# Gating row transfers by matmuls, and 128 columns of z as the weights of one matmul

## The chip, the cores and the metric

One core of one Trainium2 chip runs the kernel. The metric is the device time of one execution in microseconds (us). Engines: PE (matmul), with its weight loads shown apart as PEld, DVE (vector), ACT (scalar), POOL (GpSimd), SP (which issues most DMAs).

## The reference

A long convolution by FFT over the sequence, then a mixture of experts over the rows of its result.

```python
batch, seq, d_model = (8, 5056, 128)
...
Yf = np.fft.rfft(x, n=2 * S, axis=1) * np.fft.rfft(h, n=2 * S, axis=0)[None]
y = np.fft.irfft(Yf, n=2 * S, axis=1)[:, :S, :]
...
x = y.reshape(B * S, D)                       # 40448 rows of 128
g_idx = np.argmax(x @ w_group, axis=1)        # one of 4 groups
e_idx = np.argmax(xg @ w_expert[g], axis=1)   # one of 4 experts of the group
out[tok] = g_w * e_w * (np.maximum(x @ w1[g, e], 0.0) @ w2[g, e])
```

## The kernel before, in words

The transform of length 2S = 10112 = 158 x 64 is made by matmuls with constant matrices, in three rounds; round 0 holds the filter and two batches, rounds 1 and 2 three batches each (`ROUNDS`, `nu` = 2, 3, 3).

- `stage1(r)` makes the transform over n1 (48 loads, two steps each; L427 in four tiles of 64x64, L433 with 128 columns of weights).
- `groups(r)` takes 40 pairs of frequencies two at a time: `forward` (L531), `multiply` by the filter (L549), `add` (L583), `inverse` over k2 (L599), whose result z is copied by ACT into `zs` (L610, L612) and stored to `zd` in DRAM.
- `side(r)` makes the inverse over n1 from `zd`, in 16 lumps. A lump does four n2: for each n2 and batch u, L734 multiplies 126 rows of `zm` as weights (64 columns, twice: `c` = 0 and 64, one for each half of PE's columns) by 79 moving columns of `ig`; L748 adds the other 32 rows; ACT copies to `yT` (L755). `zs` keeps its columns as (half r, batch u, 64 channels), so the 128 channels of one batch don't lie side by side. Every two lumps there is a group of 8 n2: gate logits (`lm`, `lt`), rows transposed into `rw` (L791, L792), and `gate_math`, which finds each row's place in the array sorted by expert (`posf`, L1003).
- A group of rows is sent to its places in DRAM (`srt`) by 10 or 15 indirect DMAs of 128 rows (L868), issued by POOL. `side` appends them to the list `self.sends`; `send()` takes one out, and it is called at many chosen places in the program. In front of each, one column of `posf` is copied to `pos` on ACT or DVE (L867). This copy lies in its engine's queue at the chosen place, and the transfer waits for it; so it sets the time of the transfer.
- `ffn_steps` are the experts, in blocks of 512 rows of 8 steps: three fp32r matmuls each for `w1` (L1374 to L1376) and `w2` (L1392 to L1394). Results go out by indirect DMAs (L1445), in the blocks of known number (`timed`) behind a copy `at` of their row numbers on ACT (L1443).

`weave` lays the parts into one program by weights: `side(0)` beside round 1, `side(1)` beside round 2, `side(2)` beside the first experts. Each engine runs its instructions in that order. A group's transfers must be issued before its `rw` buffers are used again, two groups later; `rows(0)` issues what is left then. A matmul on f32 data shows in the trace as two weight loads and two matmuls: the 1024 calls of L734 are 2048 records.

Of the kernel before, what the change touches and what calls it, by code (L numbers as in the profile page):

```python
# [232 lines left out]
class Kernel:  # L233
# [5 lines left out]
    def pools(self, ctx):  # L239
        tc = self.tc  # L240
        self.cp = ctx.enter_context(tc.tile_pool(name="cp", bufs=1))
        self.dr = ctx.enter_context(tc.tile_pool(name="dr", bufs=1, space=DRAM))
        self.ctx, self.banks = ctx, ExitStack()
        self.pq = self.banks.enter_context(tc.tile_pool(name="pq", bufs=4, space=PSUM))
        self.turns, self.beside, self.sends, self.tick = 0, "", [], 0
# [136 lines left out]
    def stage1(self, r):  # L382
# [32 lines left out]
        def mm(k):  # L415
# [7 lines left out]
            for j in range(h * QB // 2, (h + 1) * QB // 2):  # L423
                if fold:
                    for b in range(2):
                        for c in range(2):
                            nc.tensor.matmul(  # L427
                                pp[c * 64:c * 64 + 64, b, j * 2 * HALF:(j + 1) * 2 * HALF],
                                lhsT=tiles[i][b * 64:b * 64 + 64, j, c, :], rhs=self.f[b * 64:b * 64 + 64, 0:2 * HALF],
                                start=True, stop=True, tile_position=(b * 64, c * 64),  # L430
                            )
                else:
                    nc.tensor.matmul(  # L433
                        whole[:, j * 256:j * 256 + N1], lhsT=views[i][:, j * 128:j * 128 + 128], rhs=self.f,
                        start=True, stop=True,
                    )
# [34 lines left out]
    def groups(self, r):  # L471
# [42 lines left out]
        def forward(p):  # L514
# [7 lines left out]
            for i, (to, of, w) in enumerate(steps):  # L522
                for b in range(2):
                    rows = slice(b * 64, b * 64 + 64)
                    for c in range(2):
                        k = w[rows, c * 64:c * 64 + 64]
                        if p == 0 and c == 0:
                            k = first[0][rows, 256 + i * 64:320 + i * 64]
                        data = st[rows, min(2 * p + c, NG - 1)].rearrange("p t w -> p (t w)")
                        begin = to == both or p == 0 and i in (0, 2)  # L530
                        nc.tensor.matmul(  # L531
                            px[c * 64:c * 64 + 64, b, to], lhsT=k, rhs=data[:, of],
                            start=begin, stop=i == len(steps) - 1 or p == 0 and i == 1, tile_position=(b * 64, c * 64),
                        )
# [22 lines left out]
        def product(p):  # L557
# [9 lines left out]
            self.send("a")  # L567
# [8 lines left out]
            if r == 2 and p % 2 == 0 and len(self.sends) > 12:  # L576
                self.send("a")
# [9 lines left out]
        def inverse(p):  # L587
# [7 lines left out]
            for part in range(2):  # L595
                wt, k = (cgs[p + LP], 320 - part * 64) if p > 0 else (first[0], part * 128)
                for c in range(n):
                    for h in (0, 64):
                        nc.tensor.matmul(  # L599
# [6 lines left out]
            else:  # L606
                z = cx.tile([128, 2, W], F32, name="zs", bufs=3)
            if pp is None:
                for c in range(n):
                    nc.scalar.copy(out=z[:, c, 0:w], in_=pz[c][:, 0:w])  # L610
            else:
                nc.scalar.copy(out=z[:, 0:n, 0:w], in_=pp[:, 0:n, 0:w])  # L612
# [33 lines left out]
        def step(k):  # L646
# [4 lines left out]
            self.tick += 1  # L651
# [47 lines left out]
    def side(self, r):  # L699
# [27 lines left out]
        def mm(n):  # L727
# [3 lines left out]
            for u in range(nu):  # L731
                for c in (0, 64):
                    k = c * nu + u * HD
                    nc.tensor.matmul(  # L734
                        pys[q][c:c + 64, col(n, u)], lhsT=zms[q][:, n % QB, k:k + 64], rhs=self.ig[:, 0:NH],
                        start=n % QB == 0 and u == 0, stop=False, tile_position=(0, c),
                    )

        def rest(n):

            zt = zts.pop(n // 4)
            for u in range(nu):
                for q in (n // QB, n // QB + 1):
                    k = q % 2 * QB * RT
                    for c in (0, 64):
                        d = c * nu + u * HD
                        both = pys[q][c:c + 64, 0:QB * c1].rearrange("p (i u m) -> p i u m", i=QB, u=nu)[:, :, u]
                        nc.tensor.matmul(  # L748
# [4 lines left out]
            for q in (n // QB, n // QB + 1):  # L753
                k = QB * q % 8 * c1
                nc.scalar.copy(out=self.yT[:, k:k + QB * c1], in_=pys.pop(q)[:, 0:QB * c1])  # L755

        def lump(k):
            def f():
# [8 lines left out]
                rest(4 * k)  # L767

# [9 lines left out]
        def rows(i):  # L778
# [10 lines left out]
            for j in range(n):  # L789
                k = (4 * i + j) * GP  # L790
                nc.tensor.transpose(out=pt[:, j * D:(j + 1) * D], in_=self.yT[:, k:k + GP], identity=self.ident)  # L791
# [38 lines left out]
        for o in range(N2 // 8):  # L830
# [3 lines left out]
            if r < 2:  # L834
# [3 lines left out]
                at.append((t + 4.7, both(lm, lambda: rows(0)), False))  # L838
                at.append((t + 6.4, both(lt, lambda: rows(1)), False))
                at.append((t + 9.5, both(*more), False))  # L840
                at += [(t + 6.5 + 5.6 * k / (NMATH + REST), advance(ops), True) for k in range(NMATH + REST)]
                at.append((t + 12.15, lambda o=o, s=sends: self.sends.extend((8 * r + o, f, self.tick) for f in s), True))
            else:
# [4 lines left out]
                at.append((t + 3, both(lm, lambda: rows(0)), False))  # L848
                at.append((t + 4, both(lt, lambda: rows(1)), False))
                at.append((t + 5, both(*more), False))  # L850
                at += [(t + 4.02 + 3.3 * k / (NMATH + REST2), advance(ops), True) for k in range(NMATH + REST2)]
                at.append((t + 7.4, lambda o=o, s=sends: self.sends.extend((8 * r + o, f, self.tick) for f in s), True))
# [10 lines left out]
    def scatter(self, k, j, p, r, T):  # L863


        def f(copy):
            copy(out=k["pos"][:, j:j + 1], in_=k["posf"][:, j:j + 1])  # L867
# [7 lines left out]
            )  # L875
            self.no_dep(f"scatter_idx{r}", ins)
# [6 lines left out]
    def send(self, eng="v"):  # L883

        if eng == "a":
            eng = "s" if self.sends and self.sends[0][2] < self.tick else "v"
        if self.sends:
            self.sends.pop(0)[1](self.nc.vector.tensor_copy if eng == "v" else self.nc.scalar.copy)
# [5 lines left out]
    def gate_math(self, od, k, t0, T, nu, rest):  # L894
# [105 lines left out]
        posf = tl([], "posf", bufs=2)  # L1000
# [3 lines left out]
        k["posf"] = posf  # L1004
        k["pos"] = cx.tile([128, 15], I32, name="pos", bufs=3)[0:P, 0:T]
        yield
# [353 lines left out]
    def mm1(self, j, i):  # L1360
# [9 lines left out]
        for f in range(i * G, i * G + G):  # L1370
# [5 lines left out]
            nc.tensor.matmul(o, lhsT=wh[:, k:k + 128], rhs=xl, start=False, stop=True)  # L1376
# [7 lines left out]
    def mm2(self, n, i, c, j=None):  # L1384
# [3 lines left out]
        for f in range(i * G, i * G + G):  # L1388
# [5 lines left out]
            nc.tensor.matmul(p, lhsT=wh[:, k:k + 128], rhs=hl, start=False, stop=f == 7)  # L1394
# [43 lines left out]
    def scatter_out(self, n, timed=False):  # L1438

        for ids, o in self.due[:n]:  # L1440
            if timed:
                at = self.fx.tile([128, 1], I32, name="at", bufs=8)
                self.nc.scalar.copy(out=at, in_=ids)  # L1443
                ids = at
# [7 lines left out]
            )  # L1452
            self.no_dep("scatter_out", ins)
# [45 lines left out]
    def ffn_steps(self, j, prev, end):  # L1499
# [22 lines left out]
        def act(at):  # L1522
            for w, k, q in plan:
# [9 lines left out]
                elif q == "o":  # L1533
                    if prev and j < NA - 2 and at in (4, 6):
                        self.put()
                        self.send("s")
# [109 lines left out]
    def run(self):  # L1646
        tc = self.tc
        with ExitStack() as ctx:
            self.pools(ctx)
            with ExitStack() as c2:  # L1650
# [29 lines left out]
                for r in range(3):  # L1680
# [38 lines left out]
                for k, f in enumerate(steps):  # L1719
# [27 lines left out]
                    elif k < 8 * (NA - 2) and k % 8 not in (3, 4, 5, 6):  # L1747
                        add(lambda: self.send("s"))
# [38 lines left out]
```

## Time and profile before

| | |
|---|---|
| median of 3 runs | 1764.83 us |
| lowest and highest | 1753.78 and 1769.3 us |
| profiled execution | 1761.84 us |
| its span, from the first to the last instruction | 1760.3 us |
| mean granted clock of PE | 0.989 of full speed |

The span misses 1.5 us of the profiled execution's time. The stages in the span: round 0 ends near 140 us, round 1 runs from 140 to 400 and round 2 to 690, the experts from there. "Idle" of an engine is put down to what ended it; "issue" means that the profile shows nothing that the engine waited for.

### The profile page before, as it was taken

The page shows a single profiled execution, that of the slowest core. Times are in us where ns is not written, and L with a number is a line of the kernel's source. Part 1 is how long each engine was busy: PE and PEld are TensorE (multiplying, and loading weights), DVE is VectorE, ACT ScalarE, POOL GpSimd, SP SyncE. Part 2 cuts the span into 40 slices and gives each one's busy share as a digit, 9 for nine tenths or more (in the row PEclk, how much of TensorE's full clock was granted, in tenths as well). Part 3 has the DMA queues.
Part 4 walks back from the last instruction along what each step waited for, and adds up shares of the span by engine and source line. Part 5 has one row for each costly group of instructions (what it writes and reads, how often), then busy time and mean ns, then how long its engine had stood idle before and what let it go on. Part 6 is the DMA issues. An engine that isn't in the chain of part 4 may idle for free. (4 is left out here: it accounts for less than half of the span.)

```text
span 1760.3 us, 47512 instructions
## 1 busy us (share of the span) xinstructions
PE 1649.6 (94%) x16576; PEld 1267.6 (72%) x16576; DVE 1317.5 (75%) x2969; ACT 1118.5 (64%) x2645; POOL 763.5 (43%) x730
## 2 busy tenths in 40 slices
PE   8998898988889898999999999999999999999998
PEld 7676745546755554777777777787777877888987
DVE  6554587864567677687787778888788888887888
ACT  5554444443444444677777777677777777776876
POOL 1451232333244445325455545345555555334545
PEclk9999999998999999999999999999999999999999
DMA  7797576766666787676666755476965687555667
GB/s 212 225 289 214 161 230 215 254 204 201 176 199 212 232 242 214 176 187 178 166 177 165 176 151 142 115 177 185 213 171 138 167 216 199 141 135 147 165 159 176
DMA packets 403939, 330.22 MB, mean 188 GB/s; under 512 B 167708, under 2 KB 347425, under 8 KB 403672
## 3 DMA queue, kind: packets, MB, share of 16 engines
q1 hardware_dynamic: 374808, 271.01, 56.9%
q0 software_dynamic: 20608, 41.79, 7.3%
q10 hardware_dynamic: 8256, 14.10, 2.8%
q8 instruction: 139, 2.28, 0.6%
q14 instruction: 128, 1.05, 0.2%
HBM read 208.00 MB, written 96.86 MB: 173 GB/s over the span
## 5 line engine op out<-in xcount | busy, mean ns | idle before, releaser
L868 POOL DMA_INDIRECT srt<-rw,pos x320 | 334.0, 1044 | 491.1 <-ACT pos L867 141.0
L1445 POOL DMA_INDIRECT out<-orow,at x176 | 190.8, 1084 | 237.1 <-ACT at L1443 122.9
L549 DVE TENSOR_TENSOR y<-pp,hg 128x768 f32<-128x768 f32 (+1 forms) x108 | 92.5, 857 | 93.9 <-ACT hg L539 33.4
L1445 POOL DMA_INDIRECT out<-orow,sids x92 | 96.2, 1045 | 114.8 <-DVE orow L1412 89.3
L599 PE MATMUL pp<-y,cg 64*64 64x384 f32 (+1 forms) x1504 | 132.0, 444 | 13.2 <-issue 6.5
L531 PE MATMUL pp<-st,cg 64*64 64x192 f32 (+1 forms) x1588 | 121.5, 404 | 4.0 <-issue 1.9
L755 ACT COPY yT<-py 128x474 f32<-128x474 f32 (+1 forms) x96 | 44.7, 513 | 116.8 <-PE py L748 88.5
L612 ACT COPY zs<-pp 128x768 f32<-128x768 f32 (+1 forms) x106 | 75.6, 714 | 64.5 <-PE pp L599 38.2
L445 DVE TENSOR_TENSOR st<-pp,odd 128x320 f32<-128x320 f32 x96 | 46.9, 489 | 91.4 <-ACT odd L444 87.4
L734 PE MATMUL py<-ig,zm 126*64 126x79 f32 x2048 | 92.3, 237 | 21.6 <-issue 18.8
L734 PEld LDWEIGHTS py<-ig,zm 126*64 126x64 f32 x2048 | 78.9, 137 | 43.1 <-issue 35.1
L599 PEld LDWEIGHTS pp<-y,cg 64*64 64x64 f32 x1504 | 62.4, 132 | 61.5 <-issue 40.2
L1380 DVE SCALAR_TENSOR_TENSOR h3l<-px,h3h 128x512 fp32r<-128x512 f32 (+1 forms) x111 | 74.4, 671 | 40.9 <-ACT h3h L1379 39.1
L1380 DVE SCALAR_TENSOR_TENSOR h0l<-px,h0h 128x512 fp32r<-128x512 f32 (+1 forms) x109 | 73.3, 672 | 37.2 <-ACT h0h L1379 26.5
L531 PEld LDWEIGHTS pp<-st,cg 64*64 64x64 f32 x1588 | 66.5, 133 | 43.5 <-issue 29.6
L1379 ACT ACTIVATE h0h<-px 128x512 fp32r<-128x512 f32 (+1 forms) x109 | 64.0, 587 | 50.8 <-PE px L1376 38.0
L1380 DVE SCALAR_TENSOR_TENSOR h2l<-px,h2h 128x512 fp32r<-128x512 f32 (+1 forms) x112 | 75.3, 672 | 23.8 <-ACT h2h L1379 15.3
L549 DVE TENSOR_TENSOR m<-pp,hg 128x768 f32<-128x768 f32 (+1 forms) x108 | 91.5, 847 | 0.0
L792 ACT COPY rw<-py 128x1024 uint16<-128x1024 uint16 (+1 forms) x88 | 81.1, 938 | 16.1 <-remote 6.8
L1379 ACT ACTIVATE h3h<-px 128x512 fp32r<-128x512 f32 (+1 forms) x111 | 65.3, 589 | 32.4 <-PE px L1376 20.9
L583 POOL TENSOR_TENSOR y<-y,m 128x512 f32<-128x512 f32 x40 | 50.9, 1277 | 77.3 <-DMA hd<-hg 43.0
L1380 DVE SCALAR_TENSOR_TENSOR h1l<-px,h1h 128x512 fp32r<-128x512 f32 (+1 forms) x111 | 74.4, 671 | 11.3 <-issue 7.7
(482 smaller groups left out, 5248.3 us busy)
## 6 DMA issues: line engine op xcount, KB each, us to landing
wr<-in_moe_w SPq DMA_DIRECT2D x373, 256.0 KB
zd<-zs SPq DMA_DIRECT2D x66, 384.0 KB
zm<-zd SPq DMA_DIRECT2D x64, 378.0 KB
cg<-in_c_g SPq DMA_DIRECT2D x106, 224.0 KB
zd<-zs SPq DMA_DIRECT2D x39, 256.0 KB
hg<-hd SPq DMA_DIRECT2D x68, 128.0 KB
xt<-in_x ACTq DMA_DIRECT2D x52, 160.0 KB
zm<-zd SPq DMA_DIRECT2D x32, 252.0 KB
```

Of the source, the lines that this page charges most:

```text
L445: nc.vector.tensor_tensor(out=all_st[:, 0:2 * HALF, d], in0=even, in1=odd, op=ALU.add)
L531: nc.tensor.matmul(px[c * 64:c * 64 + 64, b, to], lhsT=k, rhs=data[:, of], start=begin, stop=i == len(steps) - 1 or p == 0 and i == 1, til ...
L549: nc.vector.tensor_tensor(out=t[:, :, 0:w].rearrange("p t (r u d) -> p t r u d", r=2, u=nu), in0=taken(px, part).unsqueeze(1).broadcast_to ...
L583: (nc.gpsimd if r == 0 else nc.vector).tensor_tensor(out=y[:, :, 0:w], in0=y[:, :, 0:w], in1=m[:, :, 0:w], op=ALU.add)
L599: nc.tensor.matmul(pz[c][h:h + 64, 0:w], lhsT=wt[c * 64:c * 64 + 64, k + h:k + h + 64], rhs=y[c * 64:c * 64 + 64, part, 0:w], start=part = ...
L612: nc.scalar.copy(out=z[:, 0:n, 0:w], in_=pp[:, 0:n, 0:w])
L734: nc.tensor.matmul(pys[q][c:c + 64, col(n, u)], lhsT=zms[q][:, n % QB, k:k + 64], rhs=self.ig[:, 0:NH], start=n % QB == 0 and u == 0, stop ...
L792: nc.scalar.copy(out=od["rw"][i // 2][:, 4 * i % RH:4 * i % RH + n, 0:2 * D].rearrange("p j (h d) -> p j h d", h=2), in_=pt[:, 0:n * D].bi ...
L868: ins = self.nc.gpsimd.indirect_dma_start(out=self.srt, out_offset=bass.IndirectOffsetOnAxis(ap=k["pos"][0:p, j:j + 1], axis=0), in_=k["rw ...
L1379: nc.scalar.activation(out=hh, in_=p, func=AF.Relu)
L1380: nc.vector.scalar_tensor_tensor(out=hl, in0=p, scalar=0.0, in1=hh.bitcast(F32), op0=ALU.max, op1=ALU.subtract)
L1445: ins = self.nc.gpsimd.indirect_dma_start(out=self.a["out"], out_offset=bass.IndirectOffsetOnAxis(ap=ids, axis=0), in_=o, in_offset=None, ...
```

## The change

1. The copies to `pos` and `at` go. `gate_math` writes the places as integers at once. Instead, each indirect DMA gets a dependency on `self.mark`, the last marked matmul in the program at the place of the call (`behind`). Matmuls of stage 1, of `forward` (for the first of two pairs after its first third, for the second at the end), `inverse`, `rest`, `rows` and the experts set the mark.
2. The places of the calls change: in stage 1 of rounds 1 and 2 after every fourth step (it was every second); in `groups` one after each product and one after each second inverse (further ones before); one after each lump and each other large piece of `side`, outside the experts (`beside`).
3. `inverse` lets ACT write z as (batch u, half r, 64 channels), and L734 takes 128 columns of one batch as the weights of one matmul over all of PE's columns. Half as many matmuls and weight loads are issued there.

```diff
@@ groups
             for i, (to, of, w) in enumerate(steps):
+                if i == 1 and p % 2 == 0:
+                    self.mark = last
...
+            if p % 2 == 1:
+                self.mark = last
...
-            self.send("a")
+            self.send()
             yield
             m = multiply(px, p, 1, "m", 2)
...
-            if r == 2 and p % 2 == 0 and len(self.sends) > 12:
-                self.send("a")
...
+            by_unit = z[:, 0:n, 0:w].rearrange("p t (u r d) -> p t r u d", r=2, d=HD)
...
-                nc.scalar.copy(out=z[:, 0:n, 0:w], in_=pp[:, 0:n, 0:w])
+                nc.scalar.copy(
+                    out=by_unit, in_=pp[:, 0:n, 0:w].rearrange("p t (r u d) -> p t r u d", r=2, d=HD)
+                )
...
                     add(p)
-                    if p == k:
-                        self.send("a")
...
-                    if r == 2 or i == 1:
-                        self.send("s")
+                    if i == 1 or len(self.sends) > 20:
+                        self.send()
@@ side
-                for c in (0, 64):
-                    k = c * nu + u * HD
-                    nc.tensor.matmul(
-                        pys[q][c:c + 64, col(n, u)], lhsT=zms[q][:, n % QB, k:k + 64], rhs=self.ig[:, 0:NH],
-                        start=n % QB == 0 and u == 0, stop=False, tile_position=(0, c),
-                    )
+                nc.tensor.matmul(
+                    pys[q][:, col(n, u)], lhsT=zms[q][:, n % QB, u * D:(u + 1) * D], rhs=self.ig[:, 0:NH],
+                    start=n % QB == 0 and u == 0, stop=False,
+                )
...
-                        d = c * nu + u * HD
+                        d = u * D + c
...
+        def beside():
+            if self.beside != "experts":
+                self.send()
...
                 rest(4 * k)
+                beside()
...
-                at.append((t + 4.7, both(lm, lambda: rows(0)), False))
+                at.append((t + 4.7, both(lm, lambda: rows(0), beside), False))
@@ scatter, send
-        def f(copy):
-            copy(out=k["pos"][:, j:j + 1], in_=k["posf"][:, j:j + 1])
+        def f():
             ins = self.nc.gpsimd.indirect_dma_start(
...
+            self.behind(ins)
...
+    def behind(self, ins):
+        if self.mark is not None:
+            info = mybir.DependencyInfo(mybir.DependencyClass.Sync, mybir.DependencyReason.DATA)
+            self.tc.add_manual_dep(ins.ins, self.mark.ins.name, info, reason="transfers are issued one by one")
@@ gate_math
-        nc.vector.tensor_tensor(out=posf, in0=posf, in1=sg, op=ALU.mult)
+        nc.vector.tensor_tensor(out=k["pos"], in0=posf, in1=sg, op=ALU.mult)
@@ scatter_out
-            if timed:
-                at = self.fx.tile([128, 1], I32, name="at", bufs=8)
-                self.nc.scalar.copy(out=at, in_=ids)
-                ids = at
...
+            if timed:
+                self.behind(ins)
@@ run
-                        if r > 0 and k % 2 == 1:
+                        if r > 0 and k % 4 == 1:
                             add(self.send)
...
-                    elif k < 8 * (NA - 2) and k % 8 not in (3, 4, 5, 6):
-                        add(lambda: self.send("s"))
+                    elif k < 8 * (NA - 2) and (k < 8 * (N0 - 2) or k % 8 not in (3, 4, 5, 6)):
+                        add(lambda: self.send())
```

## Rows read from the trace of the kernel before

**Rows 1.** Page, part 1: busy time (share of the span) xinstructions.

```profile
PE 1649.6 (94%) x16576; PEld 1267.6 (72%) x16576; DVE 1317.5 (75%) x2969; ACT 1118.5 (64%) x2645; POOL 763.5 (43%) x730
```

**Rows 2.** Busy time by stage: stretch, its us, engines, granted clock, DMA share, GB/s.

```profile
140.00:420.00 280.00, 249.01 (x4208) 167.02 (x4208) 192.64 (x476) 127.20 (x335) 79.28 (x82) 0.97 0.69 214
420.00:690.00 270.00, 238.03 (x3653) 152.67 (x3646) 179.10 (x451) 124.08 (x338) 113.97 (x111) 0.98 0.70 209
690.00:1060.00 370.00, 360.01 (x2666) 281.54 (x2667) 284.73 (x663) 269.23 (x616) 170.36 (x160) 0.99 0.68 174
1060.00:1600.00 540.00, 523.66 (x2363) 420.98 (x2363) 441.21 (x915) 404.99 (x903) 265.07 (x252) 1.00 0.63 165
```

**Rows 3.** Groups by form: busy us, mean ns, idle before and what ended it.

```profile
L734 PE MATMUL py<-ig,zm 126*64 126x79 f32 x2048 | 92.3, 237 | 21.6 <-issue 18.8 <-ACT rw L792 2.5
```

**Rows 4.** Timeline of PE, two lumps: start, us, instructions (PE's records are pipelined).

```profile
311.42 1.31 PE L734 MATMUL py<-ig,zm 126*64 126x79 f32 x32
...
763.21 0.50 PE L1394 MATMUL pz<-h0l,w2h 128*128 128x512 f32 x1
763.64 1.86 PE L734 MATMUL py<-ig,zm 126*64 126x79 f32 x48
```

**Rows 5.** Weight loads by line: least, median and largest ns, first and last start.

```profile
L734 PEld LDWEIGHTS py<-ig,zm x2048: 132/137/231, 154.0 to 1049.5; 126*64 126x64 f32 x187
...
L433 PEld LDWEIGHTS pp<-f,xt x288: 186/190/338, 6.5 to 490.4; 128*128 128x128 f32 x144
```

**Rows 6.** Timeline of PEld, the first two 128-column loads of one step.

```profile
18.30 0.30 PEld L433 LDWEIGHTS pp<-f,xy 128*128 128x128 f32 x2
```

**Rows 7.** Timeline of PE: fp32r matmuls with 128-column weights and 256 moving columns.

```profile
1690.54 0.28 PE L1374 MATMUL py<-firstx,first 128*128 128x256 f32 x1
1690.65 0.28 PE L1375 MATMUL py<-firstx,first 128*128 128x256 f32 x1
```

**Rows 8.** Timeline of POOL: indirect DMAs around 605 us [idle before <-releaser].

```profile
603.14 0.97 POOL L868 DMA_INDIRECT srt<-rw,pos  x1 [0.30 <-ACT te L918]
604.42 0.99 POOL L868 DMA_INDIRECT srt<-rw,pos  x1 [0.30 <-issue]
...
608.28 0.97 POOL L868 DMA_INDIRECT srt<-rw,pos  x1 [0.30 <-issue]
```

**Rows 9.** Timeline of PE in the same stretch: one lump.

```profile
604.10 0.83 PE L734 MATMUL py<-ig,zm 126*64 126x79 f32 x17
605.21 0.37 PE L734 MATMUL py<-ig,zm 126*64 126x79 f32 x4 [0.28 <-issue]
...
610.31 0.95 PE L734 MATMUL py<-ig,zm 126*64 126x79 f32 x10 [1.05 <-issue]
```

**Rows 10.** PE's waits, 140 to 420 us: us in total, times, longest us.

```profile
PE pp L427 <- ACT odd L444: 4.3, 3, 2.2
...
PE py L734 <- issue: 3.6, 8, 1.1
```

**Rows 11.** PE's waits, 420 to 690 us.

```profile
PE py L734 <- issue: 13.0, 27, 1.3
PE pp L427 <- issue: 5.1, 6, 2.3
...
PE py L791 <- issue: 0.7, 2, 0.4
```

**Rows 12.** Groups by form: the copies that go, and copies out of PSUM.

```profile
L612 ACT COPY zs<-pp 128x768 f32<-128x768 f32 x65 | 51.9, 799 | 56.4 <-PE pp L599 35.3 <-remote 10.1 <-PE py L791 7.5
...
L867 ACT CAST pos<-posf 128x1 int32<-128x1 f32 x268 | 49.2, 194 | 7.1 <-DVE posf L1003 7.1
...
L1443 ACT COPY at<-ids 128x1 int32<-128x1 int32 x176 | 33.5, 190 | 0.0
...
L450 ACT COPY st<-pp 128x632 f32<-128x632 f32 x48 | 32.9, 686 | 34.7 <-PE pp L433 22.3 <-DMA xt<-in_x 5.1 <-PE py L734 2.0
...
L612 ACT COPY zs<-pp 128x512 f32<-128x512 f32 x39 | 22.9, 586 | 6.3 <-DMA zd<-zs 2.0 <-POOL y L583 1.2 <-PE pp L599 1.2
```

More of the change, by code (lines that the diff above doesn't have):

```diff
@@ L244, in pools @@
         self.pq = self.banks.enter_context(tc.tile_pool(name="pq", bufs=4, space=PSUM))
-        self.turns, self.beside, self.sends, self.tick = 0, "", [], 0
+        self.turns, self.beside, self.sends, self.mark = 0, "", [], None
     def share(self):
@@ L426, in mm @@
                         for c in range(2):
-                            nc.tensor.matmul(
+                            self.mark = nc.tensor.matmul(
                                 pp[c * 64:c * 64 + 64, b, j * 2 * HALF:(j + 1) * 2 * HALF],
@@ L432, in mm @@
                 else:
-                    nc.tensor.matmul(
+                    self.mark = nc.tensor.matmul(
                         whole[:, j * 256:j * 256 + N1], lhsT=views[i][:, j * 128:j * 128 + 128], rhs=self.f,
@@ L598, in inverse @@
                     for h in (0, 64):
-                        nc.tensor.matmul(
+                        self.mark = nc.tensor.matmul(
                             pz[c][h:h + 64, 0:w], lhsT=wt[c * 64:c * 64 + 64, k + h:k + h + 64],
@@ L790, in rows @@
                 k = (4 * i + j) * GP
-                nc.tensor.transpose(out=pt[:, j * D:(j + 1) * D], in_=self.yT[:, k:k + GP], identity=self.ident)
+                self.mark = nc.tensor.transpose(
+                    out=pt[:, j * D:(j + 1) * D], in_=self.yT[:, k:k + GP], identity=self.ident
+                )
             nc.scalar.copy(
@@ L837, in side @@
                 at.append((t + 3, lump(2 * o + 1), False))
[L838 to L840 removed]
+                at.append((t + 4.7, both(lm, lambda: rows(0), beside), False))
+                at.append((t + 6.4, both(lt, lambda: rows(1), beside), False))
+                at.append((t + 9.5, both(*more, beside), False))
                 at += [(t + 6.5 + 5.6 * k / (NMATH + REST), advance(ops), True) for k in range(NMATH + REST)]
[L842 removed]
+                at.append((t + 12.15, lambda o=o, s=sends: self.sends.extend((8 * r + o, f) for f in s), True))
             else:
@@ L847, in side @@
                 at.append((t + 2, lump(2 * o + 1), False))
-                at.append((t + 3, both(lm, lambda: rows(0)), False))
-                at.append((t + 4, both(lt, lambda: rows(1)), False))
-                at.append((t + 5, both(*more), False))
+                at.append((t + 3, both(lm, lambda: rows(0), beside), False))
+                at.append((t + 4, both(lt, lambda: rows(1), beside), False))
+                at.append((t + 5, both(*more, beside), False))
                 at += [(t + 4.02 + 3.3 * k / (NMATH + REST2), advance(ops), True) for k in range(NMATH + REST2)]
-                at.append((t + 7.4, lambda o=o, s=sends: self.sends.extend((8 * r + o, f, self.tick) for f in s), True))
+                at.append((t + 7.4, lambda o=o, s=sends: self.sends.extend((8 * r + o, f) for f in s), True))
         at.sort(key=lambda x: x[0])
@@ L1375, in mm1 @@
             nc.tensor.matmul(o, lhsT=wl[:, k:k + 128], rhs=xh, start=False, stop=False)
-            nc.tensor.matmul(o, lhsT=wh[:, k:k + 128], rhs=xl, start=False, stop=True)
+            self.mark = nc.tensor.matmul(o, lhsT=wh[:, k:k + 128], rhs=xl, start=False, stop=True)
         hh, hl = (t[:, 0:G * n] for t in self.hs[i % 4])
@@ L1393, in mm2 @@
             nc.tensor.matmul(p, lhsT=wl[:, k:k + 128], rhs=hh, start=False, stop=False)
-            nc.tensor.matmul(p, lhsT=wh[:, k:k + 128], rhs=hl, start=False, stop=f == 7)
+            self.mark = nc.tensor.matmul(p, lhsT=wh[:, k:k + 128], rhs=hl, start=False, stop=f == 7)
     def out_evac(self, n, c):
```

21 lines of the change are left out of this document (9 added, 12 removed).

## The prediction

> **What bounds the kernel now.** I read the busy shares first. PE is busy for 94% of the span, DVE for 75%, ACT for 64% [rows 1], and every engine runs a fixed order, so time given to PE or taken from it is first in line to move the end. Then the busy time by stage: PE stands idle for 31 of 280 us and 32 of 270 us in the rounds from 140 to 690 us, but only for 10 of 370 and 16 of 540 us beside the experts; the clock was granted at 0.97 or more throughout [rows 2]. So the slack that this change could find lies between 140 and 690 us.
>
> What fills it is shown by PE's own waits there. The largest heading is L734 with "issue", a wait that the profile cannot name: 13.0 us in the second stretch, 3.6 us in the first [rows 10, 11]. Ten more groups have the same heading in these two stretches (L427, L599, L531, L433, L748, L791), from 5.1 to 0.7 us, together 20.9 us [rows 11].
>
> The timelines tell what goes with it. An undisturbed lump of 48 matmuls of L734 takes 1.86 us, one of 32 takes 1.31 us [rows 4]. The lump at 604 us ran its first 17 matmuls in 0.83 us and then got four or so at a time, every 0.7 to 1.4 us, until past 611 us [rows 9]. In this stretch POOL issued indirect DMAs back to back, one each 1.28 us (0.97 us of work, 0.30 us between), with nothing to hold them [rows 8]. In other such runs L734 or L599 falters in the same way; beside single transfers I found little of it. I read it as PE's supply of instructions being held up by runs of indirect DMAs: L734 is the densest stretch, 4 instructions (two loads, two matmuls) per 0.069 us, 58 per us, so it starves first. That the runs are the cause is inferred from their being side by side.
>
> **L734's new form, undisturbed: about +42 us.** The step between two pairs follows from the two undisturbed lumps: (1.86 - 1.31) / (24 - 16 pairs) = 0.069 us [rows 4]. There are 1024 pairs, and each becomes one matmul with 128 columns of weights. Its 79 moving columns stream as fast as before, but the loads do not. A load of 64 columns shows 137 ns, one of 128 columns 190 ns [rows 5]: 53 ns for 64 columns more. In the old form the two 64-column loads of a pair go to different halves of the array side by side, and 53 ns hide behind 69 ns of streaming. In the new form a load fills about 107 ns and no longer hides. Seen directly: two 128-column loads in a row end 0.30 us after the first starts, so the second starts 0.30 - 0.19 = 0.11 us after the first [rows 6]. Matmuls with 128-column weights and 256 moving columns follow each other at 0.11 us as well, and nothing of that width is seen faster [rows 7]. I take 0.110 us: 1024 x (0.110 - 0.069) = **+42 us**. The bounds are 0 (the loads hide) and 1024 x (0.120 - 0.069) = +52 us, an estimate that adds 10 ns to the row of 0.11 us.
>
> The Trainium skill bears on this in "TensorE: Matmul & The Clock Gate". Its section "LDWEIGHTS (loading the stationary operand)" has the load take the column count over 1.2 per ns, 53 and 107 ns, which speaks against the change, and the rows agree (53 ns for 64 columns more, 110 ns from load to load). Its section "Back-to-back issue gap" gives streams of load and matmul at 128 columns as some 81 ns each. By that figure this term would be an estimated +12 us; the row of 110 ns speaks against it.
>
> Beside the experts something comes back. Before L734 starts, PE changes from the whole array to two halves: the first load starts 0.43 us after the start of L1394 [rows 4], where 512 columns need about 0.22 us (twice the 0.11 us for 256) [rows 7]. The new form needs no change there: 16 lumps x 0.2 us = **-3 us**, bounds 0 and -4.
>
> **What the stalls in L734 give back: about -27 us.** L734 holds PE for 92.3 us and lets it idle for 21.6 us [rows 3], 113.9 us. Undisturbed it would be 16 x 1.31 + 32 x 1.86 = 80.5 us. So 33 us are stalls. In the lump at 604 us some 31 matmuls and as many loads came in 6 us, about 10 instructions per us [rows 9]. The new form asks for two per 0.11 us, 18 per us, and starts with whatever PE has queued. So even a run of transfers beside it costs little, and fewer runs are expected. I take 80% of the 33 us; bounds -15 (a lump of 48 in a run would still take 48 / 10 = 4.8 us instead of 2.8 us) and -33.
>
> **What spacing the transfers gives the other lines: about -16 us.** The ten groups with 20.9 us of "issue" idle [rows 11] lose more than their idle time, since PE counts as busy while it gets a few matmuls. In L734 the ratio is 33 / 21.6 = 1.5, so these lines lose some 32 us. New places: a product every two pairs of `forward`, with marks at a third of the first and at the end of the second, an `inverse`, and the pieces of `side`. The 270 us of the second stage [rows 2] hold 20 steps of two pairs and most of a stage 1, so a step has some 10 us (an estimate) for its three calls and about two of `beside`: 2 us apart on average, above the 1.28 us of a run. But the calls of `beside` fall anywhere between the others, and `rows(0)` still sends leftovers together behind one mark. I take half; bounds 0 and -32.
>
> **The copies that go: about -3 us.** ACT loses 268 copies (49.2 us) and 176 (33.5 us) [rows 12], 83 of its 1118 us [rows 1]; the remaining copies, some of them on DVE, are of the same kind. None lies on PE's path by itself. PE waits for ACT and DVE in few places (the largest, L427 for `odd`, 4.3 us [rows 10]); 7% less work on ACT takes a few us of it. Bounds 0 and -8. The new order of z in `inverse` costs ACT nothing: a copy of 512 elements takes 586 ns, one of 768 takes 799 ns, which gives 686 ns for 632; L450, which rearranges its 632 elements, takes 686 ns [rows 12]. The added waits stand on POOL. Behind a waiting transfer there only further transfers are queued, and the clearing of borrowed input tiles in stage 1; each mark lies earlier in PE's order, so nothing waits in a circle. If a transfer comes so late that ACT waits for its `rw` buffer, that costs 1.28 us for each transfer left over.
>
> **The sum.** 1761.8 + 42 - 3 - 27 - 16 - 3 = 1754.8, so **1755 us**, against the profiled execution's own 1761.8 us. The median shown is 1764.8 us, 3 us above it, so this is 0.6% under the median. A difference of 1% (17 us) is about what a measurement of this kernel can tell.
>
> **The rivals.**
> - *The stalls stay (slower).* If the faltering belongs to something that the spacing doesn't touch, such as other traffic on the DMA engines, which are 70% busy in these rounds [rows 2], L734 keeps its 33 us and pays 39 us more: 1761.8 + 42 - 3 - 3 = 1798 us. For it: the runs are side by side with the stalls, no more. Against it: undisturbed lumps lie in the same rounds under the same DMA load. It decides where lumps of L734 still take twice an undisturbed 2.0 or 2.8 us (1.31 + 16 x 0.041, 1.86 + 24 x 0.041). Chance 0.14.
> - *The transfers aren't spaced.* Neighbouring marks, or leftovers behind one mark, keep runs of three and more. L734 is spared by its lower rate, the other lines are not: 1755 + 16 = 1771 us. Chance 0.19.
> - *More comes back.* The idle time of PE from 140 to 1600 us is 89 us [rows 2]; without the 21.6 and 20.9 us already counted, 47 us are left, mostly waits for ACT and DVE. If runs hold those up too, half of it goes with them: 1755 - 23, about 1732 to 1735 us. Chance 0.17.
> - *The loads hide.* At 0.069 us per matmul the +42 us are gone: 1713 us. Beside it stands the figure of 81 ns from "Back-to-back issue gap" in the Trainium skill's TensorE page: by an estimate from it 1755 - 30 = 1725 us. Chance 0.05, since no row shows 128 columns under 0.11 us.
>
> **How the numbers follow.** The sum's case has 0.45: 0.14 of it more than 1% faster, 0.29 within, 0.02 slower. Faster: 0.14 + 0.17 + 0.05 = 0.36. Slower: 0.02 + 0.14 + 0.04 from the second rival = 0.20. Within 1%: 0.29 + 0.15 = 0.44. The range reaches from the third rival's 1732 to 1786 us, which takes in the second with its 1771 and some of the terms' bounds; it leaves out the first and the fourth, 0.19.
>
> **What would show it.** L734 with 1024 records at a step of 0.11 us, lumps of about 2.0 and 2.8 us, none of 5 us; its weight loads near 190 ns. L868 on POOL waiting for PE, with gaps of 2 us or more between most transfers and hardly a run of three. "Issue" waits of PE on L599, L531 and L427 between 140 and 690 us at half or less. No L867 and L1443 on ACT, L612 at 799 ns as before. I would be wrong if lumps step at 0.07 us, if lumps still falter, or if ACT waits for `srt` before `rw`.

## The result and the profile after

| | before | after |
|---|---|---|
| median of 6 runs | 1765.39 us | 1742.41 us |
| lowest and highest | 1753.78 and 1769.3 us | 1734.62 and 1748.04 us |
| ratio after/before, 95% interval | | 0.9865 [0.9835, 0.9894] |
| profiled execution | 1761.84 us | 1737.86 us |

The kernel is 1.35% faster. The forecast of 1755 us is 13 us too high; the time lies inside the range of 1732 to 1786. In the profiled execution the gain is 24 us, and it shows before the experts: the first expert matmul (L1374, now L1386) starts at 670.5 us, before at 696.8, 26 us earlier. From there to the start of the last one it takes 1057.5 us, before 1055.6, although L736 holds PE 10.9 us longer there than L734 did (44.8 and 33.9 us, busy and idle time together).

Lines move in the changed kernel: L734 is L736, L748 is L750, L599 is L601, L531 is L533, L612 is L617, L868 is L876, L1374 to L1394 are L1386 to L1406; L427 stays.

The page's first part answers to [rows 1]: PE has 1024 instructions and ACT 500 less.

```profile
PE 1654.3 (95%) x15552; PEld 1291.9 (74%) x15552; DVE 1310.3 (75%) x2917; ACT 1082.6 (62%) x2145; POOL 753.6 (43%) x730
```

Busy time by stage, as in [rows 2]. In both rounds PE is busier, by 7.7 and 9.0 us in the same stretch, and gets further: more of the program fits in.

```profile
140.00:420.00 280.00, 256.71 (x4095) 179.41 (x4092) 193.02 (x470) 129.19 (x292) 82.95 (x84) 0.99 0.72 221
420.00:690.00 270.00, 246.98 (x3156) 164.14 (x3157) 194.22 (x469) 128.70 (x269) 119.14 (x115) 0.98 0.73 220
```

The lumps of the new form, from the timeline of PE: two batches, three batches, and one beside the experts. Against the undisturbed lumps of [rows 4] they take 0.70, 1.04 and 0.94 us more.

```profile
150.40 2.01 PE L736 MATMUL py<-ig,zm 126*128 126x79 f32 x16
...
406.77 2.90 PE L736 MATMUL py<-ig,zm 126*128 126x79 f32 x24
...
709.13 0.39 PE L1406 MATMUL pz<-h0l,w2h 128*128 128x512 f32 x1
709.36 2.80 PE L736 MATMUL py<-ig,zm 126*128 126x79 f32 x24
```

The step of a matmul is (2.90 - 2.01) / 8 = 0.111 us. Beside the experts the first matmul follows L1406's start by 0.23 us. In [rows 4] it was 0.43, but only 3 of the 16 lumps of the kernel before show that much: the median is 0.32 us, now 0.23, and the 16 sum to 5.5 us, now 4.1. The loads, as in [rows 5], are as long as other 128-column loads:

```profile
L736 PEld LDWEIGHTS py<-ig,zm x1024: 186/192/338, 150.4 to 1031.6; 126*128 126x128 f32 x171
```

Groups of PE by line (busy us, mean ns, idle before and what ended it). First the kernel before, lines not shown so far:

```profile
L599 PE MATMUL pp<-y,cg 64*64 64x384 f32 (+1 forms) x1504 | 132.0, 444 | 13.2 <-issue 6.5 <-DVE m L549 4.0 <-PE pp L599 0.9
L531 PE MATMUL pp<-st,cg 64*64 64x192 f32 (+1 forms) x1588 | 121.5, 404 | 4.0 <-issue 1.9 <-PE pp L599 1.0 <-PE pp L531 0.9
...
L427 PE MATMUL pp<-f,xt 64*64 64x80 f32 x1824 | 52.8, 246 | 16.7 <-issue 5.4 <-DMA xt<-in_h 4.1 <-ACT st L450 2.4
...
L748 PE MATMUL py<-igt,zt 64*64 64x158 f32 x1024 | 50.9, 308 | 2.2 <-issue 2.0
```

The same lines of the changed kernel, and L736, which answers to [rows 3]:

```profile
L601 PE MATMUL pp<-y,cg 64*64 64x384 f32 (+1 forms) x1504 | 124.6, 445 | 14.8 <-DVE m L553 8.6 <-issue 2.7 <-DVE cs L966 1.4
L736 PE MATMUL py<-ig,zm 126*128 126x79 f32 x1024 | 124.0, 277 | 5.3 <-ACT rw L801 3.7 <-issue 1.5
L533 PE MATMUL pp<-st,cg 64*64 64x192 f32 (+1 forms) x1588 | 119.8, 405 | 1.9 <-issue 0.9 <-PE pp L533 0.6 <-PE pp L601 0.4
...
L427 PE MATMUL pp<-f,xt 64*64 64x80 f32 x1824 | 50.5, 243 | 12.7 <-issue 4.4 <-DMA xt<-in_h 4.1 <-ACT odd L444 1.2
...
L750 PE MATMUL py<-igt,zt 64*64 64x158 f32 x1024 | 47.3, 308 | 2.2 <-issue 2.2
```

Busy and idle time together, L736 holds PE for 129.3 us against 113.9: +15.4. These four lines hold it for 5.8, 3.8, 6.3 and 3.6 us less. With the other groups of L427, L433, L531, L599, L748 and L791 the six lines of the prediction's third term hold PE 31 us less, all of it before the experts. (Records of two tiles can overlap and then count twice; with each moment counted once it is 26 us.)

What is left of the 24 us, some 8 us, comes back beside the experts. PE's waits for ACT there sum to 4.0 us, before to 15.0; the largest, before and after:

```profile
PE ptr L1408 <- ACT oT L1397: 5.9, 5, 2.3
```

```profile
PE ptr L1420 <- ACT oT L1409: 1.3, 2, 0.7
```

POOL's transfers, beside [rows 8] (idle before and its releaser in brackets): most have a gap, and runs of two and three are left. Counted before 700 us, with runs as transfers less than 1.5 us from start to start: the kernel before has 28 alone, 24 runs of two, 16 of three, 12 of four and 3 of five; the changed one 68 alone, 45 of two, 8 of three, 3 of four and one of seven.

```profile
575.45 1.47 POOL L876 DMA_INDIRECT srt<-rw,pos  x1 [1.83 <-PE pp L601]
577.22 0.98 POOL L876 DMA_INDIRECT srt<-rw,pos  x1 [0.30 <-PE pp L533]
578.50 0.99 POOL L876 DMA_INDIRECT srt<-rw,pos  x1 [0.30 <-issue]
580.87 0.98 POOL L876 DMA_INDIRECT srt<-rw,pos  x1 [1.38 <-ACT ns L509]
583.06 0.98 POOL L876 DMA_INDIRECT srt<-rw,pos  x1 [1.21 <-PE py L750]
```

PE's waits from 420 to 690 us, beside [rows 11]: of the 13.0 us of "issue" on L734, 1.3 are left.

```profile
PE pp L427 <- issue: 3.0, 6, 1.2
...
PE py L736 <- issue: 1.3, 1, 1.3
```

### The profile page after: what moved, and what is told of

Read it like the earlier page. It is cut to its first block, busy times and chain, and to the rows that moved or that the text cites. A ratio compares the mean times of both kernels' runs of the same rounds, so it can differ in the third digit from the quotient of the medians.

```text
span 1736.2 us, 44930 instructions
## 1 busy us (share of the span) xinstructions
PE 1654.3 (95%) x15552; PEld 1291.9 (74%) x15552; DVE 1310.3 (75%) x2917; ACT 1082.6 (62%) x2145; POOL 753.6 (43%) x730
## 5 line engine op out<-in xcount | busy, mean ns | idle before, releaser
L876 POOL DMA_INDIRECT srt<-rw,pos x320 | 332.2, 1038 | 455.9 <-DVE st L446 67.6
L1453 POOL DMA_INDIRECT out<-orow,ids x176 | 184.1, 1046 | 258.6 <-PE pz L1406 69.9
L601 PE MATMUL pp<-y,cg 64*64 64x384 f32 (+1 forms) x1504 | 124.6, 445 | 14.8 <-DVE m L553 8.6
L736 PEld LDWEIGHTS py<-ig,zm 126*128 126x128 f32 x1024 | 119.9, 192 | 17.3 <-issue 7.2
L736 PE MATMUL py<-ig,zm 126*128 126x79 f32 x1024 | 124.0, 277 | 5.3 <-ACT rw L801 3.7
L533 PE MATMUL pp<-st,cg 64*64 64x192 f32 (+1 forms) x1588 | 119.8, 405 | 1.9 <-issue 0.9
L617 ACT COPY zs<-pp 128x768 f32<-128x768 f32 (+1 forms) x106 | 75.7, 714 | 48.7 <-PE pp L601 35.3
L601 PEld LDWEIGHTS pp<-y,cg 64*64 64x64 f32 x1504 | 59.2, 133 | 59.0 <-issue 33.1
L533 PEld LDWEIGHTS pp<-st,cg 64*64 64x64 f32 x1588 | 61.5, 133 | 45.3 <-issue 37.0
L1391 ACT ACTIVATE h1h<-px 128x512 fp32r<-128x512 f32 (+1 forms) x111 | 65.3, 588 | 28.4 <-PE px L1388 11.7
```

The costliest lines, as they stand in the source:

```text
L533: last = nc.tensor.matmul(px[c * 64:c * 64 + 64, b, to], lhsT=k, rhs=data[:, of], start=begin, stop=i == len(steps) - 1 or p == 0 and i == ...
L601: self.mark = nc.tensor.matmul(pz[c][h:h + 64, 0:w], lhsT=wt[c * 64:c * 64 + 64, k + h:k + h + 64], rhs=y[c * 64:c * 64 + 64, part, 0:w], ...
L617: nc.scalar.copy(out=by_unit, in_=pp[:, 0:n, 0:w].rearrange("p t (r u d) -> p t r u d", r=2, d=HD))
L736: nc.tensor.matmul(pys[q][:, col(n, u)], lhsT=zms[q][:, n % QB, u * D:(u + 1) * D], rhs=self.ig[:, 0:NH], start=n % QB == 0 and u == 0, st ...
L876: ins = self.nc.gpsimd.indirect_dma_start(out=self.srt, out_offset=bass.IndirectOffsetOnAxis(ap=k["pos"][0:p, j:j + 1], axis=0), in_=k["rw ...
L1391: nc.scalar.activation(out=hh, in_=p, func=AF.Relu)
```

## The experiments

They ran on three chips, here called the second, third and fourth; which chip the first comparison ran on is not on record. The chips differ: the kernel before took 1792 us on the second, 1660 on the third and 1771 on the fourth. Each was used in one session, so what differs may belong to the chip or to the session. So each run is compared with runs of the kernel before on its own chip. "First expert" is the start of the first L1374 (L1386); stalls of the n1 inverse (waits for other engines among them) are its busy and idle time less its undisturbed lumps (old form 80.5 us, new form 16 x (2.01 + 2.90 + 2.80) = 123.4 us). "Runs of 3+" counts the runs of three and more transfers on POOL that start before the first expert matmul, and "issue" sums PE's idle time before it that the profile puts down to no engine and no transfer. In the first comparison these two were 31 and 41 us before, 10 and 17 us after.

| run | chip | median us | ratio, 95% interval | first expert us | n1 inverse us, of it stalls | runs of 3+ | "issue" us |
|---|---|---|---|---|---|---|---|
| old form, new waits | 2 | 1737.8 | 0.970 [0.967, 0.973] | 661 | 102.3, 21.8 | 10 | 23 |
| new form, old waits | 2 | 1788.4 | 0.998 [0.995, 1.001] | 701 | 132.9, 9.5 | 33 | 27 |
| runs of four | 2 | 1834.6 | 1.024 [1.021, 1.027] | 745 | 140.4, 17.0 | 38 | 43 |
| no wait | 2 | 1986.5 | 1.110 [1.106, 1.115] | 837 | 142.9, 19.5 | 21 | 86 |
| changed kernel | 3 | 1684.5 | 1.016 [1.013, 1.019] | 629 | 129.2, 5.8 | 31 | 2 |
| copies at the new places | 3 | 1683.6 | 1.014 [1.011, 1.016] | 640 | 134.6, 11.2 | 33 | 7 |
| waits at the old places | 3 | 1687.4 | 1.017 [1.014, 1.020] | 640 | 134.1, 10.7 | 29 | 3 |
| plain DMAs added | 3 | 1768.3 | 1.065 [1.061, 1.068] | 713 | 150.2, 26.8 | 30 | 14 |
| kernel before, profiled | 4 | 1767.3 | one run | 703 | 120.2, 39.7 | 33 | 34 |
| changed kernel | 4 | 1745.3 | 0.988 [0.982, 0.993] | 673 | 130.3, 6.9 | 10 | 16 |
| old form, new waits | 4 | 1722.1 | 0.975 [0.971, 0.978] | 655 | 98.2, 17.7 | 9 | 18 |
| runs of four | 4 | 1815.1 | 1.023 [1.018, 1.029] | 741 | 144.7, 21.3 | 37 | 35 |

"Old form, new waits" has the new places and lacks the copies too; "no wait" has few runs because they are long.

### One part alone (second chip)

The changed kernel with L734's old form, reading the new order of z:

```diff
+                for c in (0, 64):
+                    k = u * D + c
                     nc.tensor.matmul(
-                        pys[q][:, col(n, u)], lhsT=zms[q][:, n % QB, u * D:(u + 1) * D], ...
+                        pys[q][c:c + 64, col(n, u)], lhsT=zms[q][:, n % QB, k:k + 64], ..., tile_position=(0, c),
```

> The changed kernel with the old form of the inverse over n1: pairs of 64-column matmuls on the two halves of PE (the layout of z and all transfers as changed). Theory A (runs of indirect DMAs hold up PE's instructions; the spacing of the transfers brought the gain and the 128 columns cost PE time): undisturbed, the lumps save 48 x about 0.9 us = 40 us; some stalls return since this form is the densest stretch (0 to 15 us). 1742 - 40 + 8 = 1710, 1700 to 1722 us. Rival C (the gain comes from the new form, which asks for half as many instructions): stalls in L734 and after it return, 1755 to 1775 us.

Measured 0.970, inside theory A's range: the waits, the new places and the missing copies together gain 3% without the new form. The old form still falters (21.8 us), but keeps its cheap step. The changed kernel itself did not run on this chip.

The kernel before with the new order of z and the new L734, its copies and call places kept (the parts "inverse" and "L734" of the change's diff):

> The kernel before with the layout of z and the 128-column form alone; the transfers are gated by copies at the old places. Theory A: L734 itself moves from 114 to about 129 us of PE's time, stalls of the other lines stay: 1765 + 15 = 1780, 1768 to 1792 us. Rival C: the greater part of the gain is here, 1740 to 1755 us. Rival B (the gain comes from the copies that left ACT and DVE): as in theory A, 1780 us.

Measured 0.998, no difference clear of the noise, and outside the ranges of all three theories: by the shares of 1765 us, theory A and rival B forecast 1.002 to 1.015, rival C 0.986 to 0.994. The new form doesn't bring the gain, but it isn't the loss that theory A expected either. The undisturbed lumps cost 43 us more, and about as much comes back. Part of it is stalls that the new form avoids even among unspaced transfers: 9.5 us are left, where the old form has 33 to 40 us on the two chips on which the kernel before was profiled. It wasn't profiled on this one, so the rest can't be placed.

### More and longer runs (second chip)

The changed kernel without the wait on the mark in `scatter` (nothing else spaces the transfers then):

```diff
             ins = self.nc.gpsimd.indirect_dma_start(
...
-            self.behind(ins)
```

> The changed kernel without the wait of the transfers into the sorted array for a matmul: each goes as soon as its places are known and POOL gets to it (nothing but data orders them; the results' transfers to the output keep their wait). Theory A: runs of up to 10 or 15 in a row; L533, L601 and L750 stall as before or worse: 1742 + 25 to 60 = 1767 to 1800 us. Rival B: POOL has nothing to wait for and ACT and DVE stay free of copies, 1735 to 1745 us.

Measured 1.110, far more than the 1.001 to 1.020 that theory A forecast: its direction holds, its price for long runs was too low. Before 700 us there are 11 runs of 8 to 15 transfers. PE's granted clock is lower too, busy time by stage (columns as in [rows 2]):

```profile
140.00:420.00 280.00, 247.67 (x3314) 160.75 (x3303) 166.70 (x385) 108.41 (x251) 63.15 (x64) 0.90 0.59 184
420.00:690.00 270.00, 218.55 (x2765) 151.69 (x2761) 128.71 (x344) 89.99 (x188) 81.39 (x84) 0.83 0.52 156
```

The DMA share is lower than in the changed kernel (0.52 against 0.73) while PE stands still more (51 us of 270): so it isn't the amount of traffic over the stage. What the edit changed is when the transfers go: in long runs, and at once.

The changed kernel with every fourth call of `send` issuing four:

```diff
-    def send(self):
+    def send(self, now=False):
...
-        if self.sends:
-            self.sends.pop(0)[1]()
+        self.asked = getattr(self, "asked", 0) + 1
+        for _ in range(1 if now else 4 if self.asked % 4 == 0 else 0):
+            if self.sends:
+                self.sends.pop(0)[1]()
```

> The changed kernel with the same transfers, waits and places, but every fourth call sends four transfers and the three others none. Theory A: some 80 runs of four, each holding PE's dense lines up for 2 to 3 us while they last, half of it hidden where PE's stretch is less dense: 1742 + 30 to 80 = 1772 to 1820 us, less beside the experts. Rival B: no change, 1740 to 1745 us.

Measured 1.024, inside theory A's range. On this chip the first expert matmul comes at 661 and 701 us in the two runs above, at 745 with runs of four and at 837 without the wait: the more and longer the runs, the later.

### Which half of the gating (third chip)

The changed kernel again, then with the places of the calls kept but gated by copies on ACT instead of marks (`nc.scalar.copy` to `pos` in `scatter`, no `behind`), then with the waits kept and the calls at the places of the kernel before:

> The changed kernel again, as the control of this call: 0.9865 of the kernel before, as first measured.

> The changed kernel, its transfers into the sorted array gated by a copy of their places on ACT as before, but at the new places of the calls (results keep their wait for matmuls). If the places decide: as the changed kernel, 0.985 to 0.992 of before. If the kind of gate decides, since ACT gets to a copy at other distances than PE to a matmul: runs of three and more come back, 0.993 to 1.005. If the gain is ACT's relief from these copies (rival B): the same, 0.995 to 1.005, but with runs as few as in the changed kernel.

> The changed kernel with its waits for matmuls, but the calls at the places of before. If the places decide: runs of three to five as before, and near the run with the new form alone, 0.993 to 1.003 of before. If the kind of gate decides: near the changed kernel, 0.985 to 0.990.

The changed kernel itself is 1.6% slower than before here, outside the interval of the first comparison. The three kernels lie within 0.3% of each other, so these runs don't tell marks from places. (The 629 us of the changed kernel is from its fastest execution, 1675.6 us, and not to be held against the 640 of the others.)

Why shows in the traces, and in two ways. PE has next to no idle time without a cause to save: 2 to 7 us of "issue" before the experts, where the changed kernel has 16 and 17 on the other chips. And the transfers aren't spaced here: the changed kernel has 31 runs of three and more, as many as the kernel before in the first comparison, where the same program has 10 on the other chips. So on this chip runs cost PE next to nothing; why the marks don't space the transfers here isn't shown.

POOL's transfers beside the first lump among the experts, eight of them in a row:

```profile
651.78 1.01 POOL L1453 DMA_INDIRECT out<-orow,ids  x1 [1.46 <-PE ptr L1406]
653.10 0.98 POOL L876 DMA_INDIRECT srt<-rw,pos  x1 [0.30 <-issue]
...
660.80 1.01 POOL L876 DMA_INDIRECT srt<-rw,pos  x1 [0.30 <-issue]
```

PE in the same stretch goes from line to line without a gap:

```profile
654.32 2.80 PE L736 MATMUL py<-ig,zm 126*128 126x79 f32 x24
657.05 1.04 PE L750 MATMUL py<-igt,zt 64*64 64x158 f32 x24
658.01 0.50 PE L1386 MATMUL px<-x1h,w1h 128*128 128x512 f32 x1
```

The last run on this chip adds plain DMAs of the same rows, four in a row from ACT's queue, as a stand-in for other traffic:

```diff
+            self.rows_too.append(k["rw"][j // RH][0:p, j % RH, :])
+            if len(self.rows_too) == 4:
+                for rows in self.rows_too:
+                    self.nc.scalar.dma_start(out=self.extra[self.n_extra, 0:rows.shape[0]], in_=rows)
```

> The changed kernel, and beside it every row tile of the 320 transfers into the sorted array is written once more, by a plain DMA of the same 128 pieces of 520 bytes to a scratch array in DRAM, issued from ACT's queue four in a row. If it is the traffic of a run that holds PE up: as the run with runs of four, 2 to 4% above the changed kernel (1.005 to 1.03 of before). If it is that POOL issues indirect DMAs in a row (theory A in its narrow form): under 1% above the changed kernel, for the ACT issues and the bytes (0.986 to 0.996).

It is 6.5% slower than the kernel before and 5% slower than the changed one, but by another way: PE waits for ACT and DVE, which ACT's queue holds up while it issues (443 ns each at the median, up to 2.4 us). As a test of traffic it says nothing, the more so on a chip on which runs of indirect transfers cost next to nothing either.

```profile
PE pp L603 <- DVE m L555: 24.1, 14, 6.1
PE py L738 <- ACT rw L803: 14.9, 5, 5.3
```

### Before, after, old form and runs of four together (fourth chip)

The kernels are those of the runs above, unchanged.

> The kernel before, unchanged, profiled on this chip, so that its stalls can be seen where the other three runs are made. Theory S (the change gains by taking stalls of PE away, and a chip has them or not): if the median is near 1765 to 1790 us, L734 holds PE for 110 us or more with its idle time, and the first expert matmul comes near 697 us; if it is near 1660 us, L734 holds PE for 80.5 to 90 us and the first expert matmul comes before 630 us. Theory G (the change gains mainly by moving work of ACT off, whatever the chip): L734 near 114 us in both cases.

> The changed kernel, unchanged. Theory S: on a chip with stalls (before near 1765 us or more) 0.975 to 0.99 of before; on one without (before near 1660 us) 1.010 to 1.018. Theory G: near 0.987 on any chip; the 1.016 seen once would then be an outlier.

> The changed kernel with L734 in its old form (two matmuls of 64 columns, reading the new order of z), so only the waits, their places and the missing copies are new. Theory S: on a chip with stalls 0.965 to 0.98; on one without, the 25 to 27 us that the new form costs there are gone, so 0.995 to 1.003, equal to before, and 1.4% under the changed kernel. Theory G: 0.97 on any chip. If the old form needs the lower rate of instructions of the new one to be spared (my prediction's reading), it would not be under the changed kernel on a chip with stalls.

> The changed kernel with every fourth call of send issuing four transfers and the other three none: as many transfers, in runs of four. Theory S: on a chip with stalls 3% or more over the changed kernel (1.015 to 1.03 of before); on one without, within 1% of the changed kernel (1.010 to 1.025 of before). Theory L (what costs is that transfers come later and rw or srt is waited for, on any chip): 3% or more over the changed kernel on any chip, with PE waiting for ACT's rw.

This is a chip with stalls: L734 of the kernel before holds PE for 120.2 us, and the changed kernel has its ratio of the first comparison again. All four results lie in the ranges of theory S. Theory G (0.987 anywhere) is out by the third chip. Theory L is neither shown nor refuted by the time, since no run of four ran on a chip without stalls; against it, PE's wait for `rw` is small in that run (1.9 us before L736), while its "issue" time is 35 us against 16.

The groups of the n1 inverse in the kernel before, the changed one, and the one with the old form:

```profile
L734 PE MATMUL py<-ig,zm 126*64 126x79 f32 x2048 | 96.2, 241 | 24.0 <-issue 15.2 <-ACT rw L792 6.1 <-DMA zm<-zd 2.0
```

```profile
L736 PE MATMUL py<-ig,zm 126*128 126x79 f32 x1024 | 126.1, 279 | 4.2 <-ACT rw L801 2.1 <-issue 1.9
```

```profile
L738 PE MATMUL py<-ig,zm 126*64 126x79 f32 x2048 | 86.8, 237 | 11.4 <-issue 6.8 <-ACT rw L803 2.9 <-ACT zs L617 1.1
```

The old form saves 32 us of PE against the new one, and the kernel is 23 us faster (1722.1 against 1745.3 us; the ranges don't meet). It is the fastest of the kernels that ran on either of its two chips.

A run of seven transfers lies beside the first lump among the experts in both kernels, as on the third chip. In the changed kernel it starts at 694.25 us and PE falters after L736:

```profile
696.77 2.80 PE L736 MATMUL py<-ig,zm 126*128 126x79 f32 x24
699.50 1.45 PE L750 MATMUL py<-igt,zt 64*64 64x158 f32 x21
701.38 0.36 PE L750 MATMUL py<-igt,zt 64*64 64x158 f32 x2 [0.43 <-issue]
702.80 0.34 PE L750 MATMUL py<-igt,zt 64*64 64x158 f32 x1 [1.06 <-issue]
```

With the old form it starts at 676.69 us, and the lump itself starves after 41 of its 48:

```profile
679.34 1.99 PE L738 MATMUL py<-ig,zm 126*64 126x79 f32 x41
682.48 0.30 PE L738 MATMUL py<-ig,zm 126*64 126x79 f32 x2 [1.16 <-issue]
683.91 0.29 PE L738 MATMUL py<-ig,zm 126*64 126x79 f32 x2 [1.13 <-issue]
685.33 0.54 PE L738 MATMUL py<-ig,zm 126*64 126x79 f32 x3 [1.13 <-issue]
```

With runs of four a run of seven from 618.81 us makes `forward`, whose matmuls are longer and so fewer per us, falter too:

```profile
623.17 1.06 PE L533 MATMUL pp<-st,cg 64*64 64x384 f32 x2
624.47 0.53 PE L533 MATMUL pp<-st,cg 64*64 64x384 f32 x1 [0.24 <-issue]
625.88 0.55 PE L533 MATMUL pp<-st,cg 64*64 64x384 f32 x2 [0.88 <-issue]
627.32 0.91 PE L533 MATMUL pp<-st,cg 64*64 64x384 f32 x2 [0.89 <-issue]
```

In all three the faltering ends within 1.4 us of the run: its last transfer takes until 702.95, 685.39 and 627.52 us, and PE's last such gap ends at 704.24, 686.75 and 627.32 us.

## Why the prediction was right, and where not

- **What bounds the kernel: right.** PE stood still in the rounds because runs of indirect transfers held it up. The prediction had inferred that from their being side by side; the runs with more and longer runs of transfers show it on two chips, and the stretches above show PE faltering while a run lasts. It holds on the chips of the first comparison, the second and the fourth, and not on the third. That it is PE's supply of instructions which is held up stays a reading: no run tells it from another cause.
- **L734's form, +42 us: right.** The step is 0.111 us (0.110 predicted), the undisturbed lumps cost 123.4 - 80.5 = 43 us more, the loads don't hide. The figure of 81 ns per load and matmul, which the prediction took from the Trainium skill's "TensorE: Matmul & The Clock Gate", section "Back-to-back issue gap", does not hold for these f32 matmuls with 79 moving columns.
- **The mode change, -3 us: mis-sized.** The prediction took its price from one lump, and that one is among the dearest: over the 16 lumps 5.5 us became 4.1, so it is 1.4 us.
- **The stalls in L734, -27 us: right in size.** 5.9 of 33 us are left. Both reasons count: with the old form and the new waits 17.7 of 39.7 us are left on the fourth chip, with the form alone 9.5 us on the second.
- **The other lines' stalls, -16 us: mis-sized.** The six lines gave back 31 us (26 with each moment counted once), near its bound of 32 rather than half. The step that failed is the halving, for fear that the calls of `beside` and the leftovers of `rows(0)` would keep runs: runs of two remain, but of three and more only 10 of 31 before the experts. That runs of two cost little fits with this and isn't tested by itself. Part of these us may be the clock, for which the prediction has no term: from 140 to 420 us it was granted at 0.99, before at 0.97 [rows 2], some 5 us as an estimate (280 us x 0.02). This term makes up most of the 13 us by which 1755 was too high; the likeliest case, within 1%, became a gain of 1.35%.
- **The copies, -3 us: mis-sized, and looked for in the wrong place.** ACT's busy time fell by 36 us, not 83, since 71 of the 97 us of all the copies' records overlap records of other ACT instructions; and the prediction held that PE waits for ACT in few places, of which it named L427's 4.3 us, read from 140 to 420 us alone. Before the experts nothing came of it: PE's wait for DVE's `m` before `inverse` even grew from 4.0 to 8.6 us. Beside the experts PE's waits for ACT fell from 15.0 to 4.0 us, on the fourth chip from 16.0 to 7.1, while "issue" there grew by 7 and by 3 us. The other terms (+43, -1, -27, -31) leave some 8 us of the 24 to this. That the missing copies did it is argued, since no run changes them alone. On the second chip these waits are 19.4 us in the run that keeps the copies and 6.4 and 7.9 us in two without, but 33.9 us without the wait.
- **The rivals.** "The stalls stay" fell in the first comparison and on the fourth chip; on the third there were hardly any to take away in the changed kernel, and it came out slower there by 1.6%, or 25 us, probably for the reason by which that rival would have: the form costs and little pays it back. The sum without the two stall terms would be +42 - 3 - 3 = +36 us. This stays unproven, since neither the kernel before nor the old form was profiled on that chip. "More comes back" was near in time and in part in place: waits for ACT did fall, but beside the experts, and the greater part is the six lines' own stalls. "The transfers aren't spaced" fell on the other chips; on the third it came true in the transfers and cost nothing. "The loads hide" fell.

The prediction treated the two parts as one trade. They have opposite signs on chips with stalls: the waits, with the new places and without the copies, gain 2.5 to 3.0%, and on the fourth chip, where both kernels ran, the new form gives 1.3% of it back. The new form spares more stalls than the old one, but 11 us of them (17.7 against 6.9) don't pay for 43.

What stays open: why runs of transfers hold PE up on some chips and not on the third; how far marks, places and missing copies each bring the gain; whether the new waits cost or gain anything where there are no stalls.

## What to carry to other kernels

Where PE idles with no named cause, look at what POOL's queue does at the same time: runs of indirect transfers can starve it, and spacing them, here by waits on PE's own progress at new places, gained 2.5 to 3.0%. Halving the number of matmuls in such a stretch spares it as well, but first ask whether the wider weight load still hides: here two halves side by side took 0.069 us and one whole matmul 0.111, and what it saved in stalls did not pay for that. Time both parts alone, and on more than one chip, before taking them together.

## What was not expected of the hardware

- The same kernel took 1660, 1771 and 1792 us on three chips, 8% apart (1765 us in the first comparison), and the same change is 1.2% faster on one and 1.6% slower on another. A run of eight transfers costs PE nothing on the third chip, a run of seven stops it on the fourth.
- The same program spaces its transfers on one chip and not on another: 10 runs of three and more before the experts where PE falters beside runs, 31 where it doesn't.
- PE falters 4.6, 5.4 and 6.7 us after the start of such a run, not at once, and then gets work in steps: 1.41 to 1.44 us from one portion of one to three matmul records and their loads to the next, in L738, L750 and L533 alike. At that rate it no longer matters how dense the line is.
- Where PE starved most (no wait, 420 to 690 us), its mean granted clock was 0.83 of full speed against 0.98 in the changed kernel. Behind the stall on the fourth chip the clock was granted at 0.51 from 703.0 to 709.9 us, close to the lower of its two levels, 1.2 GHz, and matmuls of 512 columns followed each other at 0.43 instead of 0.23 us. So the matmuls behind a stall can be slowed too.
